# One decode step on Trainium2: the first half of a weight and the input row requested before the kernel's critical section

## The chip, the core and the metric

The kernel runs on one core of one Trainium2 chip. The core has a matrix engine (PE, with its weight loads shown as PEld), a vector engine (DVE), a scalar engine (ACT), a general one (POOL), a sequencer for transfers (SP), and 16 DMA engines that move data between the chip's main memory and the on-chip memory. The engines run their own instruction lists and wait for each other by semaphores. The metric is the time of one execution on the device in microseconds; the number given is the median of several runs.

## What is computed

One token goes through two branches that are added. Shapes: D = 512, 32 query heads on 8 key/value heads of width 128, a window of W = 4096 positions out of a cache of 65536, F = 1792. All data is bf16.

```python
xn = layernorm(x)                                   # x: [1, 1, 512]
# branch A: attention of one token over the last 4096 cached positions
q = (xn @ wq)                                       # wq: [512, 4096]
k, v = k_cache[:, :, Sk - W:], v_cache[:, :, Sk - W:]   # 8 heads, each used by 4 query heads
p = softmax(q @ k.T * 128 ** -0.5)
a = (p @ v) @ wo                                    # wo: [4096, 512]
# branch B: one routed expert; with one token, the routing picks that token
r = xn @ w_r
y = ((silu(xn @ w_gate) * (xn @ w_up)) @ w_down) * sigmoid(r)   # [512,1792] x2, [1792,512]
out = x + a + (xn + y)
```

Everything is read once: wq 4 MB, K and V 8 MB each, wo 4 MB, w_gate and w_up 1.75 MB each, w_down 1.75 MB, in all 30.67 million bytes.

## The kernel before, in words

The kernel is written with explicit semaphores inside one critical section (`tc.tile_critical()`, line 74); the framework adds no waits of its own there. Each engine's instructions run in the order in which they are written for that engine.

**Entry.** The program begins with a few memsets on POOL and a barrier over all engines (line 547). Then SP runs a no-op (line 74) that raises a semaphore, and every engine, SP too, has a branch (line 558) that waits for this semaphore and leads into the critical section. Nothing of the kernel's own work stands before that branch.

**Transfers.** The helper `dma` (lines 158 to 161) issues a transfer on an engine and gives it a semaphore of its own. ACT issues two small ones first: `A_x` into `xrow` (line 163) and `B_w_r` into `wr_row` (line 164), 1 KB each. SP issues all the large ones, in this order: `A_wq` in two halves of 2 MB, wq0 and wq1 (line 167); K in five parts of 1 MB, 1 MB, 2 MB, 2 MB, 2 MB (line 178); V in four of 2 MB (line 276); then, after the last q matmul, `t_qp`, since they go where wq lay, w_gate and w_up (lines 277 to 279); then, after the sixth group of K has been staged (semaphore `s_c`), wo in four chunks and w_down in five, both into the place of K. The output row is written last (line 531). Since SP runs in order, a wait of SP holds up every later transfer.

**Work.** DVE begins with three memsets (lines 191 to 193), and then, when `xrow` has landed, makes the layernorm: `bn_stats` (198), `bn_aggr` (200), a square root on ACT (202), a reciprocal (205) and `xn_row` (207). PE turns `xn_row` into a column (line 212, which also waits for POOL's identity matrix), DVE makes a dozen small constants, and then the routing factor (`wr_row`, line 234, to `gfb`, line 243). After that PE multiplies by wq: 16 matmuls per half (line 256), the first 16 when wq0 has landed, two fillers (line 251), the second 16 when wq1 has landed. ACT and DVE bring q into place (lines 262 to 273).

Then a loop over the 8 key heads: DVE copies a group of K to `kin` (`C`, line 295), PE transposes it (line 328), DVE and ACT move the result to `kT` (lines 300 and 303), PE makes the scores (line 337). Softmax follows (lines 370 to 393), then a loop over the 8 value heads (lines 397 to 452). PE then does the gate and up products (line 472) and the two last products: wo by chunks as they land (line 497), with filler matmuls (line 156) between them, and w_down by chunks (line 502). DVE and ACT make the output row (lines 528 and 529).

The lines that the change touches:

```python
ctx.enter_context(tc.tile_critical())                                   # 74
wq_sb = sb("wq_sb", [P, KT, NQ], BF16)                                  # 82
xrow = sb("xrow", [1, D], BF16)                                         # 109
t_x = dma(ac, "x", xrow[:], A_x.rearrange("a b d -> (a b) d"))          # 163
t_wq = [dma(sy, f"wq{h}", wq_sb[:, h * KH:(h + 1) * KH, :],
            wq_v[:, h * KH:(h + 1) * KH, :]) for h in range(2)]         # 167
```

Of the kernel before, what the change touches and what calls it, by code (L numbers as in the profile page):

```python
# [7 lines left out]
BF16 = mybir.dt.bfloat16  # L8
# [30 lines left out]
def kernel(  # L39
# [14 lines left out]
    nc = tc.nc  # L54
    P = 128
    D = A_x.shape[2]
    KT = D // P
# [13 lines left out]
    NQ = HQ * DH  # L71
    FC = F // 4

    ctx.enter_context(tc.tile_critical())
    W3, F1, F2, F3, F4 = 2, 2, 1, 1, 2

    sb = lambda name, shape, dt: nc.alloc_sbuf_tensor(name, shape, dt)
# [1 line left out]
    PH = P // 2  # L79
    k_sb = sb("k_sb", [P, HKV, 4, 1024], BF16)  # L80
    v_sb = sb("v_sb", [P, HKV, NT, DH], BF16)
    wq_sb = sb("wq_sb", [P, KT, NQ], BF16)
    kin = sb("kin", [P, 4, 1024], BF16)
    p_sb = kin[:, 0:2, :]
    kT = sb("kT", [P, 4, 1024], BF16)
# [20 lines left out]
    eps_t = sb("eps_t", [P, 1], F32)  # L106
    sel4 = sb("sel4", [P, 1], F32)
    junk = sb("junk", [1, 2], F32)
    xrow = sb("xrow", [1, D], BF16)
    wr_row = sb("wr_row", [1, D], BF16)  # L110
    xn_row = sb("xn_row", [1, D], BF16)
    resid = sb("resid", [1, D], F32)
# [39 lines left out]
    te, ac, ve, gp, sy = nc.tensor, nc.scalar, nc.vector, nc.gpsimd, nc.sync  # L152
# [5 lines left out]
    def dma(eng, name, out_, in_):  # L158
        s = S("d_" + name)
        eng.dma_start(out=out_, in_=in_).then_inc(s, 16)  # L160
        return (s, 16)

    t_x = dma(ac, "x", xrow[:], A_x.rearrange("a b d -> (a b) d"))
    t_wr = dma(ac, "wr", wr_row[:], B_w_r.rearrange("(a d) -> a d", a=1))
    wq_v = A_wq.rearrange("(p kt) n -> p kt n", kt=KT)
    KH = KT // 2
    t_wq = [dma(sy, f"wq{h}", wq_sb[:, h * KH:(h + 1) * KH, :], wq_v[:, h * KH:(h + 1) * KH, :]) for h in range(2)]
    TP = W // PH

    def pair(name, tile_, cache, i0, i1):  # L170
# [27 lines left out]
    a = DVE.mark(ve.bn_stats(out=stats[:], in_=xrow[:]))  # L198
# [6 lines left out]
    a = DVE.mark(ve.reciprocal(out=sml[:, 1:2], in_=sml[:, 0:1]))  # L205
# [5 lines left out]
    for kt in range(KT):  # L211
        ins = te.matmul(ps[:, 6, 256 + kt:257 + kt], lhsT=xn_row[:].rearrange("a (p k) -> a k p", k=KT)[:, kt, :],  # L212
                        rhs=ident_bf[0:1, 0:1], start=True, stop=True)
# [5 lines left out]
    with nc.allow_low_precision(reason="0/1 values are exact in bf16"):  # L219
# [4 lines left out]
                                     in_=ident_bf[:].rearrange("p (q h) -> p h q", h=2)))  # L224
# [23 lines left out]
    for kh in range(2):  # L248
# [4 lines left out]
        for hf in range(2):  # L253
            for kt in range(kh * KH, (kh + 1) * KH):
                for c in range(4):
                    ins = te.matmul(ps[32 * c:32 * c + 1, hf, :], lhsT=xnT[:, kt:kt + 1],  # L256
                                    rhs=wq_sb[:, kt, (4 * hf + c) * 512:(4 * hf + c + 1) * 512],
                                    start=(kt == 0), stop=(kt == KT - 1), tile_position=(0, 32 * c))
# [4 lines left out]
    for hf in range(2):  # L263
# [3 lines left out]
        for hl in range(4):  # L267
            ins = te.transpose(qT_ps[:, hl, :], q4[:, hf, hl * DH:(hl + 1) * DH], ident_bf[:])  # L268
# [97 lines left out]
    a = POOL.mark(gp.memset(rf, 0.0))  # L366
# [8 lines left out]
    a = DVE.mark(ve.reduce_max(out=gm[:], in_=ps[0:2, 6, 0:P].rearrange("a (q c) -> a c q", q=8), axis=AX.X))  # L375
# [13 lines left out]
    for h in range(2):  # L389
        PE.need(t_p[h])  # L390
        for k in range(8):
            ins = te.transpose(tp[:, h, k * P:(k + 1) * P], p_sb[:, h, k * P:(k + 1) * P], ident_bf[:])
# [39 lines left out]
    with te.Fori(1, 9) as i:  # L432
# [4 lines left out]
        for tl in range(4):  # L437
            ins = te.matmul(pv_ps[32 * tl:32 * tl + 32, :], lhsT=pTcur[:, tl].rearrange("p q e r -> p (q e r)"),  # L438
                            rhs=vin[:, 0].rearrange("p (q t) d -> p t q d", t=4)[:, tl],
                            start=True, stop=False, tile_position=(0, 32 * tl))  # L440
        ins.then_inc(pe_pva, 1)
        te.wait_ge(s_vb, i)
        for tl in range(4):
            ins = te.matmul(pv_ps[32 * tl:32 * tl + 32, :], lhsT=pTcur[:, 4 + tl].rearrange("p q e r -> p (q e r)"),  # L444
                            rhs=vin[:, 1].rearrange("p (q t) d -> p t q d", t=4)[:, tl],
                            start=False, stop=True, tile_position=(0, 32 * tl))
        ins.then_inc(pe_pv, 1)
        collect(psf[:, bass.ds(4 * 512 + g * 8, 8)]).then_inc(pe_col, 1)
        for _ in range(W3):
# [9 lines left out]
    a = DVE.mark(ve.reduce_sum(out=oT_f[:].rearrange("p (g j) -> p g j", g=HP),  # L459
                               in_=ps[:, 4, 8:72].rearrange("p (g u j) -> p g j u", g=HP, u=2), axis=AX.X))  # L460
# [7 lines left out]
    for m in range(2):  # L468
        PE.need(t_g if m == 0 else t_u)
        for kt in range(KT):  # L470
            for c in range(4):
                ins = te.matmul(ps[32 * c:32 * c + 1, 2 + m, 0:FC], lhsT=xnT[:, kt:kt + 1],
                                rhs=wgu[:, m * KT * F + kt * F + c * FC:m * KT * F + kt * F + (c + 1) * FC],
                                start=(kt == 0), stop=(kt == KT - 1), tile_position=(0, 32 * c))
# [6 lines left out]
    a = ACT.mark(ac.activation(out=gth4[:], in_=ps[:, 2, 0:FC], func=ACTF.Tanh, scale=0.5))  # L481
# [13 lines left out]
    def grouped(j, lhsT, w):  # L495
        c = j % 4
        return te.matmul(a_ps[32 * c:32 * c + 1, :], lhsT=lhsT, rhs=w[:, j * D:(j + 1) * D], start=False, stop=False,  # L497
                         tile_position=(0, 32 * c), skip_group_check=True)

    def by_halves(lhsT, row, stop=False):  # L500
        for c in range(2):
            ins = te.matmul(g_ps[c], lhsT=lhsT, rhs=row[:, c * HD:(c + 1) * HD], start=False, stop=stop,  # L502
                            tile_position=(0, 32 * c), skip_group_check=True)
        return ins

    for k, (j0, j1) in enumerate(wo_chunks):
        PE.need(t_wo[k])
        for j in range(j0, j1):
            ins = grouped(j, oT2[:, j:j + 1], wo_sb)
# [8 lines left out]
    for k, (j0, j1) in enumerate(wd_chunks):  # L518
        PE.need(t_wd[k])
        for j in range(j0, j1):  # L520
            ins = by_halves(hTr[:, j, 0:1], wd_sb[:, j * D:(j + 1) * D], stop=(j == FB - 1))
# [41 lines left out]
```

## Time and profile before

| What | us |
|---|---|
| median of 8 runs | 81.67 |
| lowest and highest of them | 81.39, 81.95 |
| the profiled execution's own time | 81.61 |
| its span, first instruction to last | 79.8 |
| PE busy in the span | 57.0 (71%) |
| DVE busy | 44.1 (55%) |
| ACT busy | 30.3 (38%) |
| POOL busy | 10.2 (13%) |

The profile is of one execution. Times in it count from the span's first instruction. A line of its timeline has start, length, engine, line, operation, tiles and, in brackets, how long the engine had been idle before and what ended that. An engine name with q (SPq, ACTq) is an engine's sequencer issuing a transfer. In the page's slices a digit is the busy share of a fortieth of the span in tenths. The chain of work that ended last is followed back from the end: at each step to what released it. The DMA queues moved 30.72 MB with 3178 packets, 385 GB/s on average over the span; TensorE's clock was granted at 0.957 of full speed on average, with a stretch of about half between 15.4 and 22.3.

### The profile page before, as it was taken

The numbers are of one execution on the slowest core, as the hardware profiler recorded it, in microseconds if no ns is written. First come the engines' busy times: TensorE is split into PE (matmuls) and PEld (weight loads), VectorE is DVE, ScalarE is ACT, GpSimd is POOL, SyncE is SP. The second block draws the span as 40 slices with busy tenths as digits, with TensorE's granted clock in tenths as the row PEclk, the third lists the DMA queues.
The fourth block names the chain that finished last, engine by engine and source line by source line (L and its number), as shares of the span: only waits on it lengthen the run. The fifth ranks groups of instructions, "written<-read, shape, count | busy, mean of one in ns | idle before, by whom it ended". The sixth has DMA issues, their size and how long they took to land.

```text
span 79.8 us, 1627 instructions
## 1 busy us (share of the span) xinstructions
PE 57.0 (71%) x634; PEld 29.7 (37%) x636; DVE 44.1 (55%) x96; ACT 30.3 (38%) x41; POOL 10.2 (13%) x22
## 2 busy tenths in 40 slices
PE   0010873569997997997994866888777898796750
PEld 0010401266685685685682133232222441231310
DVE  3778100176637967966963754898988159003020
ACT  1941000405477796796775061224332220000010
POOL 5930000001020220220218500000000000000000
PEclk9999999855599999999999999999999999999999
DMA  0999999999999999999999999999998999999500
GB/s 17 279 460 427 394 443 406 423 443 452 452 402 419 460 435 394 427 476 411 398 427 460 411 402 443 430 420 410 445 445 375 431 415 431 415 398 401 207 7 1
DMA packets 3178, 30.72 MB, mean 385 GB/s; under 512 B 356, under 2 KB 487, under 8 KB 999
## 3 DMA queue, kind: packets, MB, share of 16 engines
q1 hardware_dynamic: 3170, 30.67, 92.0%
q8 instruction: 2, 0.03, 0.2%
q14 instruction: 2, 0.01, 0.0%
q10 hardware_dynamic: 4, 0.00, 0.0%
HBM read 30.67 MB, written 0.00 MB: 384 GB/s over the span
## 4 chain that ended last, share of the span: by engine, by line
DMA 44%; SPq 23%; PE 16%; ACT 7%; DVE 4%; issue 2%
DMA k_sb<-in_B_w_down_dram 30%; SPq L160 23%; DMA wq_sb<-in_A_wq_dram 15%; PE ps L328 10%; ACT kT L303 6%; PE ps L337 3%; DVE kin L295 2%; PE ps L268 1%; DVE kT L300 1%; PE ps L502 1%; PE ps L256 1%; ACT q L262 1%; DVE qpad L273 1%; DVE kT L528 1%; SPq L558 0%
## 5 line engine op out<-in xcount | busy, mean ns | idle before, releaser
L303 ACT COPY kT<-ps 128x1024 bf16<-128x1024 bf16 x19 | 18.6, 1016 | 9.7 <-PE ps L328 9.7
L328 PE MATMUL ps<-perm_bf,kin 128*128 128x128 bf16 x256 | 19.1, 234 | 1.3 <-DVE kin L295 0.9
L328 PEld LDWEIGHTS ps<-perm_bf,kin 128*128 128x128 bf16 x256 | 16.2, 105 | 5.7 <-issue 4.5
L295 DVE COPY kin<-k_sb 128x2048 bf16<-128x2048 bf16 x16 | 10.9, 685 | 3.0 <-PE ps L328 1.7
L300 DVE COPY kT<-ps 128x1024 bf16<-128x1024 bf16 x13 | 9.0, 691 | 4.3 <-PE ps L328 3.7
L337 PE MATMUL ps<-kT,qAB 128*32 128x512 bf16 x68 | 7.2, 414 | 1.9 <-ACT kT L303 1.9
L423 ACT CAST pvS<-ps 128x512 bf16<-128x512 f32 x8 | 4.7, 585 | 10.0 <-PE ps L429 10.0
L288 POOL COPY qAB<-qpad 128x64 bf16<-128x64 bf16 x8 | 3.6, 445 | 33.1 <-PE ps L337 33.1
L156 PE MATMUL ps<-zmov,zst 128*128 128x512 bf16 x25 | 6.6, 381 | 0.2 <-issue 0.2
L403 DVE COPY vin<-v_sb 128x2048 bf16<-128x2048 bf16 x8 | 5.5, 685 | 1.1 <-PE ps L438 0.9
L409 DVE COPY vin<-v_sb 128x2048 bf16<-128x2048 bf16 x8 | 5.5, 682 | 0.0
L438 PE MATMUL ps<-vin,pTcur 128*32 128x512 bf16 x32 | 3.2, 386 | 2.6 <-ACT pvS L423 2.2
L529 ACT CAST kT<-ps 1x256 bf16<-1x256 f32 x1 | 0.4, 363 | 12.2 <-PE ps L502 12.2
L450 PE MATMUL ps<-zmov,zst 128*128 128x512 bf16 x16 | 4.7, 376 | 0.0
L273 DVE COPY qpad<-ps 128x16 bf16<-128x16 bf16 x4 | 0.5, 168 | 6.6 <-PE ps L268 6.6
L256 PE MATMUL ps<-wq_sb,xnT 128*1 128x512 bf16 x32 | 2.9, 499 | 1.6 <-DMA wq_sb<-in_A_wq_dram 1.6
L212 PE MATMUL ps<-ident_bf,xn_row 1*128 1x1 bf16 x4 | 0.3, 166 | 4.8 <-POOL qAB L189 4.8
L516 DVE TENSOR_TENSOR kT<-ps,kT 128x512 f32<-128x512 f32 x1 | 0.7, 693 | 5.3 <-PE ps L497 5.3
L444 PE MATMUL ps<-vin,pTcur 128*32 128x512 bf16 x32 | 3.2, 387 | 0.3 <-DVE vin L409 0.2
L337 PEld LDWEIGHTS ps<-kT,qAB 128*32 128x32 bf16 x68 | 1.9, 93 | 4.1 <-issue 1.8
L262 ACT CAST q<-ps 128x512 bf16<-128x512 f32 x2 | 1.1, 588 | 5.9 <-PE ps L256 5.9
L438 PEld LDWEIGHTS ps<-vin,pTcur 128*32 128x32 bf16 x32 | 1.1, 92 | 6.0 <-DVE vin L403 5.5
(95 smaller groups left out, 55.0 us busy)
## 6 DMA issues: line engine op xcount, KB each, us to landing
v_sb<-in_A_v_cache_dram SPq DMA_DIRECT2D x4, 2048.0 KB, 40.0
k_sb<-in_A_k_cache_dram SPq DMA_DIRECT2D x3, 2048.0 KB, 24.1
wq_sb<-in_A_wq_dram SPq DMA_DIRECT2D x2, 2048.0 KB, 9.5
k_sb<-in_A_wo_dram SPq DMA_DIRECT2D x4, 1024.0 KB, 33.7
k_sb<-in_A_k_cache_dram SPq DMA_DIRECT2D x2, 1024.0 KB, 14.7
wq_sb<-in_B_w_gate_dram SPq DMA_DIRECT2D x1, 1792.0 KB, 43.8
wq_sb<-in_B_w_up_dram SPq DMA_DIRECT2D x1, 1792.0 KB, 47.7
k_sb<-in_B_w_down_dram SPq DMA_DIRECT2D x2, 512.0 KB, 34.2
```

The costliest lines, as they stand in the source:

```text
L156: te.matmul(ps[:, 7, :], lhsT=zst[:], rhs=zmov[:], start=True, stop=True)
L160: eng.dma_start(out=out_, in_=in_).then_inc(s, 16)
L295: ve.tensor_copy(out=kin[:, 2 * h:2 * h + 2, :], in_=k_sb[:, g, 2 * h:2 * h + 2, :]).then_inc(s_c[h], 1)
L300: ve.tensor_copy(out=kT[:, b, :], in_=tp[:, b, :]).then_inc(s_ev[b], 1)
L303: ac.copy(out=kT[:, b, :], in_=tp[:, b, :]).then_inc(s_ev[b], 1)
L328: ins = te.transpose(tp[:, b, k * P:(k + 1) * P], kin[:, b, k * P:(k + 1) * P], perm_bf[:])
L337: ins = te.matmul(sc[32 * cq:32 * cq + 32, e, :], lhsT=qAB[:, e, :], rhs=kT[:, b, :].rearrange("d (k h q) -> d h k q", h=2, q=PH)[:, e], s ...
L403: ve.tensor_copy(out=vin[:, 0].rearrange("p (q k) d -> p q (k d)", q=4), in_=v_in[:, :, 0:4 * DH]).then_inc(s_va, 1)
L409: ve.tensor_copy(out=vin[:, 1].rearrange("p (q k) d -> p q (k d)", q=4), in_=v_in[:, :, 4 * DH:]).then_inc(s_vb, 1)
L423: ac.copy(out=pvS[:].rearrange("p t d -> p (t d)"), in_=pv_ps).then_inc(s_pvs, 1)
L438: ins = te.matmul(pv_ps[32 * tl:32 * tl + 32, :], lhsT=pTcur[:, tl].rearrange("p q e r -> p (q e r)"), rhs=vin[:, 0].rearrange("p (q t) d ...
L450: te.matmul(ps[:, 7, :], lhsT=zst[:], rhs=zmov[:], start=True, stop=True)
```

## The change

`wq_sb` and `xrow` are now allocated before the critical section, and two transfers are issued there: wq0 on SP and x on ACT. They have the same semaphores as before. The framework is told to add no semaphore and no dependence of its own to them, and a fence is declared on SP behind them. Inside the section, ACT issues only w_r and SP begins with wq1.

```diff
+    wq_sb = nc.alloc_sbuf_tensor("wq_sb", [P, KT, NQ], BF16)
+    xrow = nc.alloc_sbuf_tensor("xrow", [1, D], BF16)
+    KH = KT // 2
+    wq_v = A_wq.rearrange("(p kt) n -> p kt n", kt=KT)
+
+    def early(eng, name, out_, in_):
+        s = nc.alloc_semaphore("d_" + name)
+        ins = eng.dma_start(out=out_, in_=in_)
+        tc.no_tile_sem_insts.add(ins.ins.name)
+        tc.add_to_no_dep_group("early", ins.ins)
+        ins.then_inc(s, 16)
+        return (s, 16)
+
+    t_wq = [early(nc.sync, "wq0", wq_sb[:, 0:KH, :], wq_v[:, 0:KH, :])]
+    t_x = early(nc.scalar, "x", xrow[:], A_x.rearrange("a b d -> (a b) d"))
+    tc.declare_fence(nc.sync.nop().ins, group="early")
     ctx.enter_context(tc.tile_critical())
...
-    wq_sb = sb("wq_sb", [P, KT, NQ], BF16)
...
-    xrow = sb("xrow", [1, D], BF16)
...
-    t_x = dma(ac, "x", xrow[:], A_x.rearrange("a b d -> (a b) d"))
     t_wr = dma(ac, "wr", wr_row[:], B_w_r.rearrange("(a d) -> a d", a=1))
-    wq_v = A_wq.rearrange("(p kt) n -> p kt n", kt=KT)
-    KH = KT // 2
-    t_wq = [dma(sy, f"wq{h}", wq_sb[:, h * KH:(h + 1) * KH, :], wq_v[:, h * KH:(h + 1) * KH, :]) for h in range(2)]
+    t_wq.append(dma(sy, "wq1", wq_sb[:, KH:, :], wq_v[:, KH:, :]))
```

What this becomes in the built program, engine by engine, after the first barrier and without the waits for data:

| Engine | before | after |
|---|---|---|
| SP | no-op (raises the entry semaphore to 1), branch, wq0, wq1, K ... | wq0, semaphore step (to 1), no-op (waits for 1, raises to 2), branch, wq1, K ... |
| ACT | branch, x, w_r, table load ... | x, branch, w_r, table load ... |
| POOL, DVE, PE | branch, work | branch, work |

The branches wait for 1 before and for 2 after. All other instructions stand in the same order on every engine.

## The prediction

> **What bounds the kernel now.** I read four views in this order: the page's slices, the chain of work that ended last in order of time, the timeline of the first microseconds, and the timeline of the places where an engine waits for a transfer. First the page: its DMA row (busy tenths in 40 slices of 2 us) and the chain's shares.
>
> ```profile
> DMA  0999999999999999999999999999998999999500
> ...
> DMA 44%; SPq 23%; PE 16%; ACT 7%; DVE 4%; issue 2%
> ```
>
> The DMA engines are full from the second slice to the 37th, so 30.67 MB in one unbroken stream set the length; no compute engine is above 71%. What matters is when this stream starts, whether it ever breaks, and what lies behind its end. The chain in order of time (start us, us, what) shows the start:
>
> ```profile
> 0.67 0.05 issue
> 0.72 0.01 SPq L74
> 0.73 0.07 issue
> 0.80 0.03 SPq L558
> 0.83 0.13 issue
> 0.96 0.40 SPq L160
> 1.36 0.06 issue
> 1.42 11.73 DMA wq_sb<-in_A_wq_dram
> ...
> 52.88 23.57 DMA k_sb<-in_B_w_down_dram
> ```
>
> At 0.67 the program's first barrier lets SP go. Then come a no-op (L74), a branch (L558) and at 0.96 the first wq request: 0.29 us from release to request, of which the no-op, the branch and the gaps round them are all there is. The chain then runs through wq's landing, and it ends on w_down: the fourth of its five pieces lands at 76.46, the last at 76.85. The SPq 23% in between is SP issuing into a full queue (7.85 us for one request at 36.08), which delays nothing while the stream is full.
>
> Now who starts when (start us, us, engine, line, what):
>
> ```profile
> 0.90 0.50 ACTq L160 DMA_DIRECT2D xrow<-in_A_x_dram  x1
> ...
> 0.96 0.87 SPq L160 DMA_DIRECT2D wq_sb<-in_A_wq_dram  x2
> 1.01 0.06 DVE L191 MEMSET eps_t<- 128x1 f32 x1 [1.01 <-SPq L74]
> ...
> 1.44 0.22 ACTq L160 DMA_DIRECT2D wr_row<-in_B_w_r_dram  x1
> ...
> 2.27 0.63 DVE L198 BATCH_NORM_STATS2 stats<-xrow 1x6 f32<-1x512 bf16 x1
> ```
>
> The trace's packets put the first wq packet at 1.98, which is 1.02 us after its request, and x's packet at 1.85, 0.95 us after its own. x has landed at 2.19, wq's halves at 8.27 and 13.15. From 2 us on about 16 packets are in flight all the time.
>
> **The change, part by part.** *The first wq request moves ahead of the no-op and the branch.* An instruction that follows a released wait starts 0.05 us after it (0.67 to 0.72 here). So the request starts at 0.72 instead of 0.96: **0.24 us earlier**. Bounds: 0.29 at most, since it stays behind the barrier; nothing at least, if the first packet is bound to something other than the request. I take 0.24, because x and wq0 show nearly the same delay from request to packet (0.95 and 1.02), each counted from its own request; the first packet then is at 1.74.
>
> *The second wq request.* SP now does the request (0.40), the fence's semaphore step, the no-op, the branch. With the chain's steps (0.06 after a request, about 0.06 each for two small steps, 0.03 and 0.13 at the branch) wq1 is requested at 0.72 + 0.40 + 0.06 + 0.12 + 0.06 + 0.16 = 1.5, against 1.42. What hides this: wq0's 2 MB keep the engines busy to 8.0, so k, v and the rest are queued as before, and the stream stays unbroken from its earlier start. All later requests depend on SP's place in the queue (full) or on PE and DVE (gate and up after the q matmuls at 13.8, wo after the sixth staging of K at 34.28), each long before its bytes are due: gate lands at 58, wo's first chunk at 64.8. Cost nothing; without that cover it is 0.1.
>
> *The other engines enter later.* Their branches wait for SP's no-op, which now stands behind a 0.40 us request and one semaphore step. It moves from 0.72 to about 1.26, so POOL, DVE and PE start **0.54 us later**. Behind DVE's branch are three memsets and the layernorm: bn_stats at 2.27 becomes 2.81, and the first wq matmuls go from 8.72 to 9.26. On ACT the x request goes ahead from 0.90 to 0.72 and takes 0.50; the branch follows at about 1.30 and w_r is requested near 1.44, as now, so its table load stays put. Whether this 0.54 costs anything is read from where the consumers wait for transfers:
>
> ```profile
> 13.19 1.03 PE L256 MATMUL ps<-wq_sb,xnT 128*1 128x512 bf16 x16 [1.63 <-DMA wq_sb<-in_A_wq_dram]
> ...
> 23.05 0.69 DVE L295 COPY kin<-k_sb 128x2048 bf16<-128x2048 bf16 x1 [1.31 <-DMA k_sb<-in_A_k_cache_dram]
> ...
> 67.36 0.60 PE L497 MATMUL ps<-k_sb,oT 128*1 128x512 bf16 x8 [0.26 <-DMA k_sb<-in_A_wo_dram]
> ...
> 69.86 0.60 PE L497 MATMUL ps<-k_sb,oT 128*1 128x512 bf16 x8 [0.49 <-DMA k_sb<-in_A_wo_dram]
> ...
> 75.85 0.49 PE L502 MATMUL ps<-k_sb,hTr 128*1 128x256 bf16 x6 [0.35 <-DMA k_sb<-in_B_w_down_dram]
> ```
>
> The bracket is idle time that ended with a landing: cover for a late compute chain. PE waits 1.63 us for wq's second half. The chain is 0.54 later and the landing 0.24 earlier, so 1.63 - 0.78 = 0.85 us of cover remain and from 12.95 on everything runs 0.24 earlier than now. Cost nothing.
>
> *The tail* (last landing 76.85, casts, output request, closing barrier: 79.8 - 76.85 = 2.95) is untouched.
>
> *Sum.* The profiled execution took 81.61, its span 79.8, with 1.81 around it. 79.8 - 0.24 = 79.56; + 1.81 = 81.37. That execution is 0.06 below the median of the eight runs (81.67), so the predicted time is 81.67 - 0.24 = **81.43 us**, -0.29%. This kernel's measurement can tell about 0.2%, that is 0.16 us, from no change.
>
> [...] Row first: w_r, requested at 1.44, had its packet only at 5.06 and its landing at 6.03, while x, requested 0.06 us before wq0, had its packet after 0.95 us. Now x and wq0 are requested at the same moment (both released within 0.01 us), so x may fall behind wq's packets. [...]
>
> **Rivals.** *(a) The earlier start is lost in a slow start.* The DMA rate is 393 GB/s in 2.0:2.5, 66 in 2.5:3.0, 393 in 3.0:3.5, 262 in 3.5:4.0 and some 430 after that; wq's first packets take 1.18 to 1.41 us, later ones 0.61. If this slow phase belongs to the clock on the wall (memsets and a table load run in it) and not to the stream's first packets, the stream gains 0.24 us at half rate or nothing: 0.12 to 0, 81.55 to 81.67, within 0.2%. For it: only one stream start is in the trace. Against: the slow packets are each engine's first.
>
> *(b) Slower: x loses the race and lands with wq0.* Landing 8.27 - 0.24 = 8.03 instead of 2.19, so the chain through bn_stats is 5.8 us late. Covers before the end: 1.63 - 0.24 = 1.39 at wq1, 1.31 at K, 0.26 + 0.49 + 0.49 at wo, 0.15 + 0.35 + 0.15 at w_down, together 4.59; fillers between them are fixed. The end is 5.8 - 4.59 = 1.2 later on a stream that is 0.24 earlier: +1.0, **82.6**. It decides only when x lands later than 2.19 + 4.59 + 0.24 = 7.0. If x only fares as w_r did (landing 4.59 after its request, at 5.3) the chain is 3.1 late, and wq1 and K take 2.7 of it; the rest goes at wo. Then the time is the forecast's.
>
> *(c) More than the shift.* If the slow first packets come from x, wq0, wq1 and w_r being set up together, wq0 alone might start at the later pace (0.61 instead of 1.25): 0.6 more, 80.8; a part of it, 81.1.
>
> *(d) The change doesn't do what it says:* the request ends up behind the no-op after all. The built order has it ahead, with no wait, so I fold this into (a).
>
> **How the numbers follow.** Forecast 81.43: 0.62, by itself 81.32 to 81.52 (shift 0.17 to 0.29, and some 0.05 of the median's own scatter). (a) 81.55 to 81.67: 0.27. (b) 82.6: 0.07. (c) 81.1: 0.04. Faster by over 0.2%: 0.56 of the forecast, 0.02 of (a), 0.04 of (c) = 0.62. Within: 0.06 + 0.24 = 0.30. Slower: 0.07 of (b) and 0.01 of (a) = 0.08. Range: from just under the forecast's own low end to the high end of (a), 81.27 to 81.70; (b) and (c) are left out, 0.11, and a little scatter.
>
> **What would show it.** In the profile after: wq0 requested near 0.72, x beside it; the first wq packet at 1.74; wq1 landed at 12.9 and the last w_down piece at 76.6, all 0.24 earlier; bn_stats near 2.8 and PE's wait for wq1 down from 1.63 to about 0.85; the distance from last landing to end still 2.95. A wq0 landing that stays at 8.27 is (a). A bn_stats after 4 is the lost race, and after 7 it is (b). What would make the prediction wrong beyond these: a break in the DMA row, or one DMA engine ending later than now against the others.

## The result, and the profile after

| | before | after |
|---|---|---|
| median us (runs) | 81.67 (31) | 81.43 (11) |
| lowest to highest | 81.39 to 81.95 | 81.33 to 81.67 |
| profiled execution, its span | 81.61, 79.8 | 81.46, 79.6 |

Ratio 0.9973, interval 0.9963 to 0.9984, that is 0.13 to 0.30 us: a small gain, but clear of no change. All medians here are of fast executions; one of four with seven memsets (84.47) and one of twelve with seven requests (89.31) ran in a slower state and are left out. To three decimals the spans are 79.816 and 79.580, 0.24 us apart.

The slices of the changed kernel's page: the DMA row is as full as it was and ends in the same slice. The chain's shares by engine are word for word those of before.

```profile
DMA  4899998999999999999999999999999999999500
...
DMA 44%; SPq 23%; PE 16%; ACT 7%; DVE 4%; issue 2%
```

Its timeline at the start:

```profile
0.73 0.41 SPq L81 DMA_DIRECT2D wq_sb<-in_A_wq_dram  x1
0.74 0.51 ACTq L81 DMA_DIRECT2D xrow<-in_A_x_dram  x1
1.44 0.21 ACTq L174 DMA_DIRECT2D wr_row<-in_B_w_r_dram  x1
...
1.50 0.33 SPq L174 DMA_DIRECT2D wq_sb<-in_A_wq_dram  x1
1.54 0.06 DVE L202 MEMSET eps_t<- 128x1 f32 x1 [1.54 <-SPq L90]
...
2.80 0.62 DVE L209 BATCH_NORM_STATS2 stats<-xrow 1x6 f32<-1x512 bf16 x1
```

wq0 is requested at 0.73 in place of 0.96, everybody else enters 0.53 us later (DVE 1.54 for 1.01), w_r's request stays at 1.44, and wq1's goes from 1.42 to 1.50. The trace's packets: the first one of wq at 1.76 in place of 1.98, the last w_down landing at 76.62 in place of 76.85. Between, a transfer's first pieces land some 0.22 us earlier (wq0's at 7.66 for 7.88) and most transfers' last pieces 0.14 to 0.17. From the last landing to the end it is 2.96 us, as before (2.97).

And where the compute engines meet the stream:

```profile
13.05 1.88 PE L267 MATMUL ps<-wq_sb,xnT 128*1 128x512 bf16 x16 [0.85 <-DMA wq_sb<-in_A_wq_dram]
...
67.20 0.60 PE L508 MATMUL ps<-k_sb,oT 128*1 128x512 bf16 x8 [0.17 <-DMA k_sb<-in_A_wo_dram]
69.69 0.60 PE L508 MATMUL ps<-k_sb,oT 128*1 128x512 bf16 x8 [0.49 <-DMA k_sb<-in_A_wo_dram]
...
75.69 0.49 PE L513 MATMUL ps<-k_sb,hTr 128*1 128x256 bf16 x6 [0.34 <-DMA k_sb<-in_B_w_down_dram]
```

PE still waits for wq1, 0.85 us now, and for wo and w_down as before. At the first of these places the wait swallows the late entry: these matmuls start at 13.05 in place of 13.19. They then take 1.88 us in place of 1.03, which is taken up again below.

One view misleads here: the chain in order of time.

```profile
1.34 0.03 SPq L569
1.37 0.13 issue
1.50 11.50 DMA wq_sb<-in_A_wq_dram
```

It begins at the entry and wq1's request at 1.50, as if the late entry still set the start. But wq1 needs 11.5 us because wq0 is moved first (landed at 8.11); wq1's landing went from 13.15 to 13.00 although its request became later. A chain names the request of the transfer that was waited for, not the queue ahead of it.

### The profile page after: what moved, and what is told of

It is laid out like the page before. It is cut to its first block, busy times and chain, and to the rows that moved or that the text cites. A ratio compares the mean times of both kernels' runs of the same rounds, so it can differ in the third digit from the quotient of the medians.

```text
span 79.6 us, 1628 instructions
## 1 busy us (share of the span) xinstructions
PE 57.3 (72%) x634; PEld 29.6 (37%) x636; DVE 44.2 (56%) x96; ACT 30.3 (38%) x41; POOL 10.0 (13%) x22
## 4 chain that ended last, share of the span: by engine, by line
DMA 44%; SPq 23%; PE 16%; ACT 7%; DVE 4%; issue 2%
DMA k_sb<-in_B_w_down_dram 30%; SPq L174 23%; DMA wq_sb<-in_A_wq_dram 14%; PE ps L339 9%; ACT kT L314 7%; PE ps L348 3%; PE ps L267 2%; DVE kin L306 2%; PE ps L279 1%; DVE kT L311 1%; PE ps L513 1%; DVE qpad L284 1%; DVE kT L539 1%; SPq L569 0%
## 5 line engine op out<-in xcount | busy, mean ns | idle before, releaser
L339 PE MATMUL ps<-perm_bf,kin 128*128 128x128 bf16 x256 | 18.5, 230 | 1.2 <-DVE kin L306 0.9
L339 PEld LDWEIGHTS ps<-perm_bf,kin 128*128 128x128 bf16 x256 | 15.7, 104 | 5.5 <-issue 4.3
L267 PE MATMUL ps<-wq_sb,xnT 128*1 128x512 bf16 x32 | 3.8, 620 | 0.9 <-DMA wq_sb<-in_A_wq_dram 0.9
## 6 DMA issues: line engine op xcount, KB each, us to landing
k_sb<-in_A_k_cache_dram SPq DMA_DIRECT2D x2, 1024.0 KB, 14.5
```

What stands on the lines that cost most here:

```text
L339: ins = te.transpose(tp[:, b, k * P:(k + 1) * P], kin[:, b, k * P:(k + 1) * P], perm_bf[:])
```

## The experiments

Theories: **start** (the stream begins 0.24 us earlier, and nothing else counts) against **layernorm** (the gain is x's earlier request), **slow start** (rival a) and **late entry** (the compute chain's lateness counts). The medians of the kernel before, taken again beside each group of experiments, were 81.69 both times; ratios are to these.

**1. wq0 alone ahead; x inside the section again.**

```diff
-    t_x = early(nc.scalar, "x", xrow[:], A_x.rearrange("a b d -> (a b) d"))
...
+    t_x = dma(ac, "x", xrow[:], A_x.rearrange("a b d -> (a b) d"))
     t_wr = dma(ac, "wr", wr_row[:], B_w_r.rearrange("(a d) -> a d", a=1))
```

> The changed kernel, but x is requested inside the critical section again; wq0 alone stays ahead of it. Start theory (the stream of transfers begins 0.24 us earlier, nothing else counts): the whole gain stays, 81.43 us, ratio to before 0.997; the first wq packet near 1.76 and the last w_down landing near 76.6. x is now requested at about 1.4 behind wq0's packets, so it may land near 5, and the layernorm starts up to 3 us later; by the covers read from the profile of before (4.6 us in all) this costs nothing. Layernorm theory (the gain is that x is requested earlier): the gain is gone, 81.67 or more.

Median 81.51, ratio 0.9973 (0.9954 to 0.9992): the ratio of the change. Its timeline shows x's lost race, then the later chain:

```profile
6.64 0.68 DVE L209 BATCH_NORM_STATS2 stats<-xrow 1x6 f32<-1x512 bf16 x1 [3.76 <-DMA xrow<-in_A_x_dram]
...
15.34 1.88 PE L267 MATMUL ps<-wq_sb,xnT 128*1 128x512 bf16 x16
...
69.56 0.60 PE L508 MATMUL ps<-k_sb,oT 128*1 128x512 bf16 x8 [0.28 <-DMA k_sb<-in_A_wo_dram]
```

x, requested at 1.44 behind wq0, lands at 6.62 and DVE idles 3.76 us for it. PE no longer waits for wq1, but at wo's third chunk it waits again: the lateness is gone. First packet 1.76, last landing 76.49. The layernorm theory falls: x 4.4 us later than before, and the gain stays.

**2. x alone ahead; wq0 inside, with the fence.**

```diff
...
-    t_wq = [early(nc.sync, "wq0", wq_sb[:, 0:KH, :], wq_v[:, 0:KH, :])]
...
-    t_wq.append(dma(sy, "wq1", wq_sb[:, KH:, :], wq_v[:, KH:, :]))
+    t_wq = [dma(sy, f"wq{h}", wq_sb[:, h * KH:(h + 1) * KH, :], wq_v[:, h * KH:(h + 1) * KH, :]) for h in range(2)]
```

> The changed kernel, but wq0 is requested inside the critical section again, first on SP; x alone stays ahead, and so does the fence on SP. Start theory: SP has one more small step ahead of wq0, which goes from 0.96 to about 1.05, so the time is 81.67 + 0.1 = 81.77, ratio 1.001. Layernorm theory: the gain stays, 81.43, ratio 0.997.

Median 81.75, ratio 1.0008 (0.9996 to 1.002): no gain. wq0's request is at 1.05, its first packet at 2.09, the last landing at 77.11. A cost of 0.1 us is in line with this and not resolved. What is excluded is a gain of 0.24 us.

**3. The kernel before, SP's requests alone delayed.**

```diff
+    s_idle = S("s_idle")
+    for _ in range(8):
+        sy.sem_inc(s_idle, 1)
     t_wq = [dma(sy, f"wq{h}", ...
```

> The kernel before, with eight semaphore steps on SP (on a semaphore that nobody waits for) ahead of wq0, inside the section: only SP's requests are later, by about 8 x 0.065 = 0.5 us; all other engines and x start as before. Start theory: 1:1, 81.67 + 0.5 = 82.2, ratio 1.006. Slow-start theory (the first packets are slow until about 3 us whatever the request's time): less than half of it, 81.7 to 81.9, ratio 1.001 to 1.003.

Median 82.16, ratio 1.0066 (1.005 to 1.0082). The request moved from 0.96 to 1.48 and the first packet from 1.98 to 2.52; the time rose by 0.47 against the 81.69 beside it. Start of stream and time go 1:1 within the interval (+0.41 to +0.67 us), in both directions, and the first packets, now from 2.52 on, still took 1.1 to 1.5 us. So the slow start moves with the stream and rival (a) falls.

**4. Seven requests ahead: both halves of wq and all of K** (run twice, the second time beside the changed kernel). `k_part`, a helper whose lines are left out here, requests a part of K by `early`.

```diff
...
+    t_wq.append(early(nc.sync, "wq1", wq_sb[:, KH:, :], wq_v[:, KH:, :]))
+    t_k = sum([k_part(a, b) for a, b in ((0, 1), (1, 2), (2, 4), (4, 6), (6, 8))], [])
...
-    t_wq.append(dma(sy, "wq1", wq_sb[:, KH:, :], wq_v[:, KH:, :]))
...
-    t_k = sum([pair("k", k_sb, A_k_cache, a, b) for a, b in steps([0, 1, 2, 4, 6, 8])], [])
```

> The changed kernel with both wq halves and all five K requests ahead of the section, seven requests on SP in place of one. SP reaches the entry about 0.46 + 5 x 0.66 = 3.8 us later, and DVE, POOL, PE and ACT's table load with it: about 4.3 us later than in the kernel before. Start theory with the covers of 4.6 us: the stream starts as in the changed kernel, so 81.43 to 81.5, ratio 0.997 to 0.998. If the covers are not real and a late compute chain counts from the first half microsecond on: about 85.

Median 81.33, ratio 0.9962 (0.9947 to 0.9977), with bn_stats at 6.54 in place of 2.27. The second run and the changed kernel beside it:

> The changed kernel once more, beside the next one on the same chip: 81.43, ratio 0.997.

> The kernel with seven requests ahead of the section, beside the changed kernel on the same chip. Start theory: its first request is at the same moment, so no difference: 81.43, ratio 0.997. If the lower median of its first run (81.33) is real, by the later requests reaching the queue without a branch between them: 81.33, ratio 0.996.

Change again: 81.43, 0.9966 (0.9953 to 0.9978). Seven ahead: 81.51, 0.9979 (0.9966 to 0.9992). The 81.33 did not come again: between seven requests ahead and one no difference is shown, and no version here is shown to be better than the change.

**5. and 6. The compute chain late by dose**, in the changed kernel, requests untouched: DVE repeats a memset five or seven times ahead of the layernorm.

```diff
+    for _ in range(5):      # 7 in the second
+        DVE.need(DVE.mark(ve.memset(ps[:, 0:2, :].rearrange("p a b -> p (a b)"), 0.0)))
     t_ps0 = DVE.mark(ve.memset(ps[:, 0:2, :].rearrange("p a b -> p (a b)"), 0.0))
```

> The changed kernel with five more of DVE's 0.91 us memsets of the same psum banks, each waiting for the one before, ahead of the layernorm: about 5 us, so bn_stats goes from 2.8 to about 7.8, 5.5 later than in the kernel before; the requests stay. By the covers as read from the profile of before (4.6 us and the 0.24 that the stream is ahead) the end is 0.7 later than before, 82.3. By what the run with seven requests ahead showed (its q was 2.8 us late and its softmax only 0.5, so the K stage hides about 1.1 more than I had read) the end is not later: 81.4 to 81.6.

> The same with seven such memsets, about 7 us: bn_stats near 9.8, 7.5 later than in the kernel before. By the covers as read from the profile of before: 81.67 + 7.5 - 4.6 - 0.24 + 0.24 less the stream's lead, some 84.3. By covers 1.1 larger: 83.2. If a late compute chain were hidden whatever its size: 81.43.

(The first estimate for seven is the changed kernel's 81.43 + 7.5 - 4.6 = 84.3; its formula is written awkwardly.) A memset with its wait took 1.20 us, more than I had counted. Five: 81.42, ratio 0.9977 (0.9956 to 0.9999), no loss. Seven: 83.13, ratio 1.0169 (1.0144 to 1.0195), with the first packet still at 1.76 and the last w_down landing at 76.55. That this is near the second estimate is luck: the kernel was 8.93 late at bn_stats, not 7.5, and with that the covers of 5.7 (4.6 and 1.1) would give 81.43 + 8.93 - 5.7 = 84.7. With five (6.52 late) they would give 82.3, where 81.42 was measured. The covers are larger than both estimates had them. The end of the chain in order of time, first with five, then with seven:

```profile
73.35 0.53 PE ps L510 x8
73.89 0.54 PE ps L170 x2
74.42 2.33 PE ps L515 x32
76.77 0.41 DVE kT L541
```

```profile
75.58 0.53 PE ps L510 x8
76.11 0.54 PE ps L170 x2
76.65 2.07 PE ps L515 x32
78.74 0.41 DVE kT L541
```

With five, PE's own run of 32 matmuls comes out just behind the last landing (76.41). With seven, it starts at 76.65, when everything has landed: PE sets the end and the stream no longer does. The page with seven shows it too: the DMA row is empty in the last three slices, where the changed kernel's is empty in two.

```profile
DMA  5699999999999999999999999999999999997000
```

Lateness against the kernel before, at four places (us; from the timelines):

| | bn_stats | q in place | max of the scores | first wo matmul | median |
|---|---|---|---|---|---|
| before, starts at | 2.27 | 15.85 | 43.74 | 66.50 | 81.67 |
| the change | +0.53 | +0.67 | -0.07 | -0.08 | 81.43 |
| x behind wq0 (1) | +4.37 | +2.76 | +0.35 | +0.35 | 81.51 |
| seven requests ahead (4) | +4.27 | +2.89 | +0.48 | +0.48 | 81.33 |
| five memsets (5) | +6.52 | +4.90 | +2.49 | +2.49 | 81.42 |
| seven memsets (6) | +8.93 | +7.12 | +4.72 | +4.71 | 83.13 |

In the last four rows 1.4 to 1.8 us is swallowed up to q, 2.4 in the K stage, in the V stage nothing, and behind it, in the last row, 4.71 less the 1.53 by which the span is longer than that of the kernel before, about 3.2.

## Why the prediction was right, point by point

*What bounds the kernel: right.* The end follows the start of the stream 1:1 within the interval: with the first packet 0.54 us later (2.52 for 1.98, experiment 3) the time rose by 0.47, with the request 0.23 earlier (0.73 for 0.96) it fell by 0.24.

*The step of the request: right.* 0.72 forecast, 0.73 found; first packet 1.74 forecast, 1.76 found; 0.24 forecast for the time, 0.24 found (81.67 to 81.43). With an interval of 0.13 to 0.30 us, agreement to the hundredth is luck.

*wq1 at 1.5: right,* and hidden by wq0 as said: it landed at 13.00 in place of 13.15.

*The late entry costs nothing: right.* The lateness was 0.53 at bn_stats but 0.63 at the first wq matmul (9.35 for 8.72), since `xn_row` took 1.10 us in place of 0.98. PE's wait for wq1 came out at 0.85, as forecast, because two errors of 0.1 cancel: PE was ready 0.64 late and not 0.54, and wq1 landed 0.15 earlier and not 0.24. One step did not hold, that from there on everything runs 0.24 earlier: the 16 matmuls behind that wait took 1.88 us in place of 1.03, so q was 0.67 late. The K stage took that up, and not by a wait for K but by PE's pace (under rival (b)).

*The race of x: it was not lost.* x was requested 0.004 us after wq0 and still had its packet first (1.73, landed 2.07). Experiment 1 shows what losing it is worth: x's packet at 5.63 and its landing at 6.62, well before wq0 had landed (8.24). w_r fared alike in the kernel before (packet 5.06, landing 6.03, wq0 8.27) and in the changed one (5.65, 6.61, 8.11). That x would land with wq0, at 8.03, the term from which rival (b)'s 82.6 is worked out, no run here shows.

*Rival (b) was priced too high.* The ledger of covers, 4.59 us, is the term that was mis-sized. Seven memsets are 8.93 late and cost 83.13 - 81.43 = 1.70, so the covers are 7.2. By place, counted from the kernel before (7.4, the stream's lead included): up to q 1.8 where I had 1.63, in the K stage 2.4 where I had one wait of 1.31, behind the V stage 3.2 where I had 1.9. Behind the V stage some of that is PE: its wo and w_down groups, not waiting any more, run closer (1.03 for 16 matmuls in place of twice 0.60); the rest stays open there. x landing with wq0, 5.8 late, would have cost nothing; five memsets, 6.5 late, did not.

In the K stage the mechanism was wrong and not only the size. PE's first and fifth group of 16 transposes of K, in the kernel before, the changed kernel and experiment 1:

```profile
16.76 1.89 PE L328 MATMUL ps<-perm_bf,kin 128*128 128x128 bf16 x16 [0.95 <-DVE kin L295]
...
25.05 1.06 PE L328 MATMUL ps<-perm_bf,kin 128*128 128x128 bf16 x16
```

```profile
17.44 1.89 PE L339 MATMUL ps<-perm_bf,kin 128*128 128x128 bf16 x16 [0.95 <-DVE kin L306]
...
25.06 1.06 PE L339 MATMUL ps<-perm_bf,kin 128*128 128x128 bf16 x16
```

```profile
19.52 1.07 PE L339 MATMUL ps<-perm_bf,kin 128*128 128x128 bf16 x16 [0.95 <-DVE kin L306]
...
25.48 1.06 PE L339 MATMUL ps<-perm_bf,kin 128*128 128x128 bf16 x16
```

From the first of these groups to the fifth it takes 8.29 us in the kernel before, 7.62 in the changed kernel, and 5.96 in experiment 1 and with seven requests, five and seven memsets alike. From the fifth to the max of the scores it is 18.6 to 18.7 in all of them. So 2.33 of the 2.41 us lie between these groups, where PE is slow at first in the two early kernels (1.89 us a group, 1.07 from 23.18 and 21.78 on) and runs at 1.07 throughout in the late ones. The chain of the kernel before goes through PE and ACT here and through no landing of K: DVE's wait of 1.31 lies beside it.

*Rivals (a) and (c):* (a) fell in experiment 3. (c) is not seen: the first packets still take 1.0 to 1.7 us.

## What to carry to other kernels

Where the transfers are one unbroken stream, as they are here (eights and nines in the DMA row from the second slice to the 37th), and their bytes and order stay as they are, the first request and what follows the last landing (2.96 us here) are left to win. In this kernel every step ahead of the first request counted in full, even 0.24 us of entering a section (81.67 to 81.43), and putting seven requests ahead in place of one added nothing that could be seen (81.51 beside 81.43). Holding up all the other engines by half a microsecond for this (0.53 here) was free, since PE waits for the stream later: it still had 0.85 us to wait for wq1. How much they may be late is better measured by a dose than added up from the waits of one profile: here the sum of the waits gave 4.6 us and the doses 7.2, and one of the waits that was added up lay beside the chain.

## What the runs showed that I had not expected

The q matmuls of one and the same kernel run at two speeds. The line of the wq matmuls, shortest, median and longest in ns, in the first and in the second run of the kernel with seven requests ahead:

```profile
L276 PE MATMUL ps<-wq_sb,xnT x32: 380/609/634, 13.0 to 17.0; 128*1 128x512 bf16 x32
```

```profile
L276 PE MATMUL ps<-wq_sb,xnT x32: 584/631/634, 13.1 to 17.1; 128*1 128x512 bf16 x32
```

In the first some matmuls took 380 ns, in the second none took less than 584. The kernel before and the changed one differ in the same way (377/482/634 and 583/631/634), and as the second 16 started 0.14 earlier and took 0.85 longer, this is the 0.7 us by which q came later. It is not shown to be the change's doing: experiment 3, the kernel before with SP alone delayed, has 583/631/634 too.

The granted clock of the views is no sure sign of this pace. In 9:14.5 it is shown as 1.00 in the changed kernel, where the wq matmuls took 583 to 634 ns, and in 16:24 as 0.61 in the kernel before and 1.00 in the changed one, though both begin their transposes there at 1.89 us a group. The number of slow matmuls differs between the two runs of the kernel with seven requests: the last four of 32 took 380 ns in the first, none in the second. What sets it no run here shows.

A small request's place beside a large one counted for much here. In experiment 3, w_r was requested 0.04 us ahead of wq0 and had its packet 0.85 us after the request, at 2.29. In the kernel before it was requested 0.48 us behind wq0 and had its packet 3.62 us after the request, at 5.06.
